# The attention's output bank in thirds, x turned by DMA, and the order of the instructions planned anew

## Chip, cores and metric

One core of one Trainium2 chip. The metric is the device time of one launch in microseconds (us); lower is better. TensorE is called PE (PEld its weight loads), VectorE DVE, ScalarE ACT, GpSimd POOL; SP issues most of the DMAs.

## What is computed

Attention with rotary positions for 4 batches x 8 heads, 576 positions and 64 values per head, then two layers with a gate between two products:

```python
q_rot, k_rot = (rotate(q), rotate(k))
scores = scale * np.matmul(q_rot, k_rot.transpose(0, 1, 3, 2))
attn = np.exp(scores - np.max(scores, axis=-1, keepdims=True))
attn = attn / (np.sum(attn, axis=-1, keepdims=True) + 1e-09)
x = np.matmul(attn, v)            # then heads side by side: 2304 tokens x 512
h = x @ w_in                      # layer 1: 512 -> 2048 -> 512
x = (h * np.clip(h + 3, 0, 6) / 6) @ w_out
h = x @ w_in2                     # layer 2: the gate is P(h) / (Q(h) + 1e-6)
out = g2(h) @ w_out2
```

To keep accuracy, float32 values are split into a high and a low float16 half in attention and layer 1 (high x high, high x low and low x high are multiplied), and into two float32r halves in layer 2.

## The kernel before, in words

**Attention.** The heads are taken in 16 pairs (4 batches of 4 pairs). A pair has five *units* (`unit`, line 820): four of 128 query rows for both heads, and a last one for the remaining 64 rows of each. A unit is a chain: PE makes the scores (L848) in one of two halves of a PSUM area; DVE takes the row maximum (L854); POOL or DVE scales it (L856); ACT takes exp in two calls (L861); POOL, ACT or DVE makes the high half p16h, DVE the low half p16l (L873); SP turns both by DMA transposes in blocks of 128 x 128 (L870), because the probabilities have to lie with the keys on the partitions; then PE multiplies them with V (L887 and L890, 30 matmuls, below called a P·V group). V has a column of ones, so that the sum of the row comes out as a 65th column. Both p16h and p16l have two buffers (`PR["p16"]`, L865).

**The output bank.** All P·V groups write the tile `ob`, one PSUM bank of 512 columns. Units are joined into *parts*: part 0 is the first two units of a pair, part 1 the other three. Unit n of a part writes 130 columns at n x 130, so a part fills up to 390. Beyond column 400 the same bank takes small products (L652, L760) that sum a column over the partitions, read by DVE (L599). When the last unit of a part is done, `x_out` (L894) normalises it: DVE makes the factor (L905), the divisor (L906) and its reciprocal (L908), and multiplies out of PSUM into the tile xn in SBUF (L910); PE transposes xn in 2 or 3 blocks into a PSUM tile `h` (L919, in float32, with the unit matrix); ACT or DVE makes the high half xt from it, DVE the low half (L923). The next part's P·V groups write the same columns, and the plan has them wait until L910 has read the bank:

```python
        op("P", c_pe(D + 1, 30), pv, r=[th, tlo, v9], w=[(ob, 0)])
```

**Layer 1** (`layer1`, L929) follows for each batch in the same two parts, 256 and 320 tokens: 16 groups of 12 matmuls (L953), with an elementwise chain on ACT, DVE (L957 to L962) and POOL or ACT for the high half, then 4 groups of 48 (L977), whose result goes to DRAM. Weights of layer 1 come in as float64 words and are decoded and split on ACT, DVE and POOL in the first 150 us; those of layer 2 are decoded later and kept in DRAM. **Layer 2** (L1114) starts when attention and layer 1 have given back their memory: five blocks of up to 512 tokens, matmuls at L1127 and L1160.

**The order.** Nothing is scheduled by the chip: each engine and each DMA queue works its own list in the order in which it was written. `Plan` collects all operations with the tiles they read and write, a cost per engine they may run on (`c_act`, `c_dve`, `c_pe`, ...), and a priority, which is a due time in ticks of 4 us plus an offset per tile name (`o_...`, in the first batch also `z_...` of the table `PR`). `order` (L388) then plays the kernel through with these costs, always giving a free engine the ready operation with the lowest priority; an engine that is not the first choice costs `pen` ticks. It counts time from an operation's end until another engine can start (L466), and `slack`. The dependences it knows go by tile and key: `(ob, 0)` and `(ob, 400)` are different keys. Waits on the chip are then put in for every conflict of what is read and written.

Of the kernel before, what the change touches and what calls it, by code (L numbers as in the profile page):

```python
# [22 lines left out]
S = 576  # L23
# [14 lines left out]
PR = {'c01': -12.485,  # L38
 'e': 2,
 'e_dec': 'GA',  # L40
 'e_dec0': 'DA',
 'e_gh': 'GD',
# [3 lines left out]
 'e_hi': 'GD',  # L46
# [5 lines left out]
 'e_qk0': 'GAD',  # L52
# [19 lines left out]
 'e_y': 'A',  # L72
# [33 lines left out]
 'o_hx': -0.79,
 'o_ident': 39.08,
 'o_k2': 11.91,
 'o_lgh': 7.11,
 'o_lgl': -78.93,  # L110
 'o_lq': -20.68,
 'o_lr': -7.59,
 'o_ls': 18.32,
 'o_lt': 5.34,
 'o_mx': 9.72,
 'o_na': 49.46,
 'o_nat': 8.34,
 'o_ob': -0.52,
 'o_ones': 50.39,
# [5 lines left out]
 'o_pw': 25.74,
 'o_pwi': -52.17,
 'o_qal': -12.64,
 'o_qam': -4.0,
 'o_qb': -50.8,
 'o_qk16': -0.86,  # L130
 'o_qpi': -2.45,
 'o_qps': 7.54,
 'o_qpv': -10.27,
 'o_r': -11.95,
# [4 lines left out]
 'o_s': -0.76,
 'o_so': -34.31,  # L140
 'o_t': -153.93,
 'o_t0': 16.25,
 'o_t1': 8.57,
 'o_tab': 0.98,
# [62 lines left out]
 'w20': 112.413,  # L207
 'w21': 133.738,
# [46 lines left out]
 'z_pth': 1.28,
 'z_ptl': -0.54,
 'z_pw': -13.15,
 'z_pwi': 41.55,
 'z_qal': -37.21,
 'z_qam': -53.51,  # L260
 'z_qb': -22.51,
 'z_qk16': 0.19,
 'z_qpi': -65.94,
# [4 lines left out]
 'z_raw': -17.19,
 'z_ropea': -4.31,
 'z_s': 29.8,  # L270
 'z_so': -1.68,
 'z_t': -7.2,
 'z_t0': 10.22,
 'z_t1': -8.07,
 'z_tab': -21.29,
# [238 lines left out]
def c_pe(n, passes):  # L514
    return passes * (n / 2.4 + 2.5)
# [741 lines left out]
```

## Time and profile before

| | |
|---|---|
| median of 3 runs | 1212.54 us (1210.96 to 1216.21) |
| the profiled execution | 1213.46 us, its span 1211.7 us |
| PE busy | 1021.2 us (84%) |
| DVE / ACT / POOL busy | 942.9 / 660.8 / 210.5 us |
| granted TensorE clock, mean | 0.932 of full |
| DMA | 137.72 MB, 276519 packets, 224192 of them under 512 B |

How to read it: the busy times are of one execution, the span runs from its first to its last instruction, and what lies between the span and its own time (1.8 us) is before and after. A wait is idle time of an engine just before an instruction, put down to what came last; idle time of an engine that sets no end costs nothing. [...] Landing is the time from issue to the last byte.

### The profile page before, as it was taken

Reading aid. Unit: us, or ns where it says so; the run is one execution under the profiler, and the core shown is the slowest. Engines: PE = TensorE matmul, PEld = TensorE weight load, DVE = VectorE, ACT = ScalarE, POOL = GpSimd, SP = SyncE. Lnnn points to the kernel's source line nnn. Section 1 sums busy time; section 2 is a strip of 40 time slices with the busy share of each in tenths; the row PEclk is TensorE's granted clock in tenths of the full one; section 3 lists DMA queues with packets and bytes.
Section 4 is the critical chain, followed back from the end, with each engine's and each line's share of the span. In section 5 each row is a group of like instructions: output and inputs, shape, how many; then the busy total and the mean of one; then the engine's idle time right before and its main releaser. Section 6 shows DMA issues by size and latency. Waiting matters only on the chain.

```text
span 1211.7 us, 21452 instructions
## 1 busy us (share of the span) xinstructions
PE 1021.2 (84%) x8182; PEld 810.7 (67%) x8182; DVE 942.9 (78%) x1697; ACT 660.8 (55%) x1183; POOL 210.5 (17%) x266
## 2 busy tenths in 40 slices
PE   0243589789889699798898998999999999999997
PEld 0122477666678467676666786777888888888895
DVE  5998798888686695796883854759989888887877
ACT  4665565553463362362441441467867667676676
POOL 0341353332130330241430420000000000000000
PEclk9955799899999699899899898999999999999999
DMA  7899765984997756878756844343010020010010
GB/s 215 215 233 231 158 157 124 159 170 99 191 157 166 142 100 148 165 158 183 142 117 145 165 107 101 114 147 93 9 48 23 1 52 10 1 35 10 1 36 18
DMA packets 276519, 137.72 MB, mean 114 GB/s; under 512 B 224192, under 2 KB 257600, under 8 KB 276416
## 3 DMA queue, kind: packets, MB, share of 16 engines
q1 hardware_dynamic: 270000, 127.91, 48.5%
q10 hardware_dynamic: 6416, 8.44, 2.5%
q8 instruction: 64, 1.05, 0.4%
q14 instruction: 39, 0.32, 0.1%
HBM read 61.33 MB, written 17.83 MB: 65 GB/s over the span
## 4 chain that ended last, share of the span: by engine, by line
PE 56%; DVE 19%; DMA 9%; issue 6%; ACT 6%; SPq 2%; POOL 2%; ACTq 0%; DVEq 0%; POOLq 0%
PE ac L1160 15%; PE h L977 9%; PE hh L1127 8%; PE h L953 7%; PE hx L1127 7%; PE s L848 5%; DVE mx L854 4%; ACT e L861 3%; DVE p16l L873 3%; DMA t<-qk 2%; PE ob L887 2%; DMA w2d<-f 2%; DVE gl L962 1%; DMA ptl<-p16l 1%; DVE t L959 1%
## 5 line engine op out<-in xcount | busy, mean ns | idle before, releaser
L953 PE MATMUL h<-xt,w 128*128 128x256 f16 (+1 forms) x1536 | 209.5, 293 | 8.3 <-DVE t L959 7.6
L953 PEld LDWEIGHTS <-w 128*128 128x128 f16 x1536 | 152.1, 101 | 53.3 <-issue 11.7
L977 PE MATMUL h<-gh,w 128*128 128x256 f16 (+1 forms) x960 | 185.3, 286 | 0.0
L1160 PE MATMUL ac<-w,lgh 128*128 128x512 f32 x576 | 179.8, 393 | 3.4 <-ACT lgh L1150 3.4
L861 ACT ACTIVATE e<-s,mx,qal 128x576 f32<-128x576 f32 (+1 forms) x144 | 116.0, 833 | 121.1 <-DVE mx L854 44.4
L977 PEld LDWEIGHTS <-w 128*128 128x128 f16 x1440 | 140.0, 98 | 35.0
L848 PE MATMUL s<-t,t 128*128 128x192 f16 (+10 forms) x360 | 91.5, 309 | 63.7 <-ACT e L861 37.0
L977 PE MATMUL h<-gl,w 128*128 128x256 f16 (+1 forms) x480 | 137.2, 286 | 0.0
L854 DVE TENSOR_REDUCE mx<-s 128x2 f32<-128x1152 f32 (+1 forms) x80 | 99.3, 1245 | 42.9 <-ACT e L861 21.6
L848 PEld LDWEIGHTS <-t 128*128 128x128 f16 (+1 forms) x720 | 64.0, 112 | 98.8 <-issue 57.0
L1160 PEld LDWEIGHTS ac<-w,lgh 128*128 128x128 f32 x576 | 107.1, 188 | 27.9 <-ACT lgh L1150 5.1
L1127 PE MATMUL hh<-x,w 128*128 128x512 f32 (+1 forms) x516 | 116.0, 374 | 0.0
L1160 PE MATMUL ac<-w,lgl 128*128 128x512 f32 x288 | 114.0, 396 | 1.3 <-DVE lgl L1151 1.2
L873 DVE TENSOR_TENSOR p16l<-e,p16h 128x1152 f16<-128x1152 f32 (+1 forms) x80 | 106.4, 1331 | 9.8 <-DMA ptl<-p16l 6.7
L957 ACT ACTIVATE t<-h,half,d 128x256 f32<-128x256 f32 (+1 forms) x128 | 75.1, 587 | 64.1 <-PE h L953 61.7
L1127 PEld LDWEIGHTS hh<-x,w 128*128 128x128 f32 x516 | 91.5, 189 | 19.6
L887 PE MATMUL ob<-v,pth 128*128 128x65 f16 (+1 forms) x800 | 81.5, 206 | 19.9 <-DVE xn L910 13.3
L1127 PE MATMUL hx<-x,w 128*128 128x512 f32 (+1 forms) x444 | 97.9, 369 | 0.0
L848 PE MATMUL s<-k,t 128*128 128x192 f16 (+10 forms) x360 | 88.7, 308 | 0.0
L1127 PEld LDWEIGHTS hx<-x,w 128*128 128x128 f32 x444 | 77.4, 188 | 16.3
L532 POOL TENSOR_SCALAR p16h<-e 128x1152 f16<-128x1152 f32 (+1 forms) x56 | 71.1, 1271 | 93.8 <-DMA pth<-p16h 65.2
L856 POOL TENSOR_SCALAR mx<-mx,qal 128x2 f32<-128x2 f32 (+1 forms) x76 | 42.0, 552 | 234.9 <-DVE mx L854 207.6
(135 smaller groups left out, 1939.6 us busy)
## 6 DMA issues: line engine op xcount, KB each, us to landing
raw<-in_moe_w_in_dram SPq DMA_DIRECT2D x32, 512.0 KB, 4.8
raw<-in_moe_w_out_dram SPq DMA_DIRECT2D x32, 512.0 KB, 4.2
w2d<-f SPq DMA_DIRECT2D x32, 256.0 KB, 4.5
w2s<-w2d SPq DMA_DIRECT2D x32, 256.0 KB, 2.7
out_dram<-ob SPq DMA_DIRECT2D x36, 128.0 KB, 2.4
vnat<-in_v_dram SPq DMA_DIRECT2D x16, 256.0 KB, 3.5
nat<-in_q_dram SPq DMA_DIRECT2D x32, 128.0 KB, 2.4
nat<-in_k_dram SPq DMA_DIRECT2D x32, 128.0 KB, 3.0
```

The source lines that it names most:

```text
L532: pool.tensor_scalar(out, in_, scale, 0.0, ALU.mult, ALU.add)
L848: pe.matmul(sbank()[r0:r0 + m, x:y], lhsT=qq[:, q0:q0 + m], rhs=kk[:, kx:kx + y - x], start=(j == 0), stop=(j == 1))
L854: op("D", c_dve(n), lambda e: vec.reduce_max(mx()[:, 0, 0:g], sv().rearrange("p (g n) -> p g n", g=g), axis=AX.X), r=[s], w=[(mx, 0)])
L856: op(EN("e_mx"), {"D": 170, "G": 270}, lambda e: EL[e].tensor_scalar(mx()[:, 1, 0:g], mx()[:, 0, 0:g], al()[:, 1:2], float(LSH * np.log(2. ...
L861: op("A", c_act(n // g, 2, False), lambda e, h=h: act.activation(et()[:, h * (n // g):(h + 1) * (n // g)], sv()[:, h * (n // g):(h + 1) * ...
L873: op(EN("lo"), c_sub(n), lambda e: EL[e].tensor_tensor(lo()[:, 0:n], et()[:, 0:n], ph()[:, 0:n], ALU.subtract), r=es + [ph], w=[lo])
L887: pe.matmul(ob()[0:m, o:o + D + 1], lhsT=w, rhs=vv[:, 0], start=(z == 0 and j == 0), stop=(z == 1 and j == 4))
L953: pe.matmul(hp()[:, 0:N], lhsT=w[:, z, kk], rhs=xt()[:, kk, 0:N], start=(n == 0), stop=(n == 11))
L957: op("A", c_act(N, 2, False), lambda e, t=t, hp=hp, f=f: act.activation(t()[:, 0:N], hp()[:, 0:N], AF.Relu, bias=half(), scale=d()[:, f:f ...
L977: pe.matmul(yp()[:, 0:N], lhsT=w[:, s_, m * 128:(m + 1) * 128], rhs=gt()[:, f, 0:N], start=(f == 0 and z == 0), stop=(f == KF - 1 and z == 2))
L1127: pe.matmul(hp()[:, 0:n], lhsT=w[:, kk], rhs=xt()[:, kk, 0:n], start=(i == 0), stop=(i == 11))
L1160: pe.matmul(accs[j][i]()[0:m], lhsT=gt()[:, x:x + m], rhs=wt(), start=(f == 0 and z == 0), stop=(f == KF - 1 and z == 2))
```

## The change

1. The thirds of the bank take turns over all units, `i % 3`, whichever part they belong to, and are three keys in the plan. After each P·V group the third is copied into an SBUF tile `xu` (new, two buffers, ACT or DVE).
2. `x_out` normalises `xu` in place in SBUF, makes high and low half there (high on ACT, low on DVE), and SP turns both by DMA transposes of 2 or 3 blocks straight into the tiles that layer 1 reads. The transposes on PE, the tile xn and the reading of `h` are gone.
3. p16l has one buffer (`'p16l': 1`), p16h keeps two.
4. The plan's costs: the time between engines falls from 200, 145, 130, 90 ns (P, A, D, G) to 190, 50, 60, 50 and `slack` from 80 to 40; small DVE operations are counted with 155 ns (before 60 to 90), small products with 330 (before 60), a matmul column with 1/2.34 ns (before 1/2.4).
5. The table `PR`: nearly all offsets and due times have other values (some 200 lines), `pen` falls from 23.2 to 7.9 ticks, and the engines allowed for some steps change.

```diff
-PR = {'c01': -12.485,
+PR = {'c01': -11.047,
...
+ 'e_ev': 'AD',
+ 'e_ev0': 'AD',
...
- 'e_hi': 'GD',
+ 'e_hi': 'GAD',
...
- 'e_w': 'GA',
+ 'e_w': 'G',
...
- 'e_xh': 'AD',
+ 'e_xh': 'A',
...
- 'e_y': 'A',
+ 'e_y': 'AD',
...
+ 'p16l': 1,
- 'pen': 23.208,
+ 'pen': 7.889,
...
- 'slack': 80,
+ 'slack': 40,
...
-                        end += (0 if o.dma else {"P": 200, "A": 145, "D": 130, "G": 90}.get(e, 0)) + PR["slack"] * (e != "N")
+                        end += (0 if o.dma else {"P": 190, "A": 50, "D": 60, "G": 50}.get(e, 0)) + PR["slack"] * (e != "N")
...
-    return passes * (n / 2.4 + 2.5)
+    return passes * (n / 2.34 + 2.5)
...
-    op("D", 140, lambda e: vec.memset(obank()[64:128, 4 * (D + 1):6 * (D + 1)], 1.0), w=[(obank, 0)])
...
-        ph, lo = (tl("attn", [128, 2 * S], F16, "p16" + z, PR["p16"]) for z in "hl")
+        ph, lo = (tl("attn", [128, 2 * S], F16, "p16" + z, n_) for z, n_ in (("h", PR["p16"]), ("l", PR["p16l"])))
...
-        o0 = (cc - 2 * part) * 2 * (D + 1)
+        o0 = i % 3 * 2 * (D + 1)
+        if cc == 2 * part:
+            xus[P, part] = tl("attn", [128, 3, 2, D + 1], F32, "xu", 2)
+        xu = xus[P, part]
...
-        op("P", c_pe(D + 1, 30), pv, r=[th, tlo, v9], w=[(ob, 0)])
+        op("P", c_pe(D + 1, 30), pv, r=[th, tlo, v9], w=[(ob, i % 3)])
+        op(EN("e_ev"), c_copy(2 * (D + 1), 0, False), lambda e: copy(
+            e, xu()[:, cc - 2 * part].rearrange("p h d -> p (h d)"), ob()[:, o0:o0 + 2 * (D + 1)]),
+           r=[(ob, i % 3)], w=[(xu, cc)])
...
-            xts[b_, part] = [tl("attn", [128, HP, PARTS[part][1]], F16, f"xt{part}{i}") for i in range(2)]
+            xts[b_, part] = [tl("attn", [128, HP, m * 128], F16, f"xt{part}{i}") for i in range(2)]
...
-            return obank()[:, 0:2 * m * (D + 1)].rearrange("p (j d) -> p j d", j=2 * m)
+            return xu()[:, 0:m].rearrange("p j h d -> p (j h) d")
...
-        xn = tl("attn", [128, 3, 2, D], F32, "xn")
         op("D", c_dve(m * 128), lambda e: vec.tensor_tensor(
-            xn()[:, 0:m].rearrange("p j h d -> p (j h) d"), ov()[:, :, 0:D],
-            r()[:, 0:2 * m].unsqueeze(2).to_broadcast([128, 2 * m, D]), ALU.mult), r=[(obank, 0), r], w=[xn])
-        tp = tl("psh", [128, 512], F32, "h", 2)
...
-                pe.transpose(tp()[:, 128 * j:128 * j + w], xn()[0:w, j].rearrange("p h d -> p (h d)"), ident()[0:w, 0:w])
-        op("P", 240 * m, turn, r=[xn, ident], w=[tp])
...
+            ov()[:, :, 0:D], ov()[:, :, 0:D], r()[:, 0:2 * m].unsqueeze(2).to_broadcast([128, 2 * m, D]), ALU.mult),
+           r=[r], w=[xu])
...
+        op(EN("e_xh"), c_copy(m * 128), lambda e: copy(e, xh()[:, 0:m], xn()[:, 0:m]), r=[xu], w=[xh])
+        op("D", c_dve(m * 128), lambda e: vec.tensor_tensor(xl()[:, 0:m], xn()[:, 0:m], xh()[:, 0:m], ALU.subtract),
+           r=[xu, xh], w=[xl])
+        for t, x in zip(xts[b_, part], (xh, xl)):
+            op("Q", (625, 189 * m, 1), lambda e, t=t, x=x: DE[e].dma_start_transpose(
+                out=t()[:, p].rearrange("p (j e) -> p j e", j=m), in_=x()[:, 0:m].rearrange("p j h d -> p (j h d)")),
+               r=[x], w=[(t, p)])
```

## Rows read from the trace of the kernel before

**Rows 1.** stages: stretch, PE, PEld, DVE, ACT, POOL, clock, DMA share, GB/s

```profile
0.00:150.00 150.00, 46.65 (x406) 33.42 (x407) 118.31 (x242) 84.61 (x170) 38.19 (x42) 0.75 0.86 211
...
150.00:745.00 595.00, 517.90 (x5574) 410.48 (x5570) 443.88 (x793) 261.69 (x440) 172.29 (x224) 0.93 0.72 148
...
745.00:1212.00 467.00, 456.67 (x2209) 366.82 (x2209) 380.72 (x663) 314.54 (x573) 0.00 (x0) 0.99 0.14 39
```

**Rows 2.** PE's waits, 150 to 745 us; columns: total us, times, longest us

```profile
PE s L848 <- ACT e L861: 31.1, 24, 3.6
...
PE h L919 <- DVE xn L910: 15.6, 8, 3.0
...
PE h L953 <- DVE t L959: 7.6, 14, 2.9
...
PE s L848 <- DVE mx L854: 5.9, 5, 2.3
```

**Rows 3.** waits of the whole run, two lines

```profile
PE ob L887 <- DVE xn L910: 13.3, 2, 11.1
...
DVE p16l L873 <- DMA ptl<-p16l: 6.7, 6, 3.0
```

**Rows 4.** busy time in ten-microsecond slices, columns as in rows 1

```profile
220.00:230.00 10.00, 6.68 (x81) 4.59 (x81) 7.05 (x12) 5.72 (x10) 3.43 (x4) 0.77 1.02 172
...
490.00:500.00 10.00, 5.45 (x77) 4.58 (x79) 7.14 (x16) 3.48 (x5) 1.68 (x3) 0.75 1.13 202
...
730.00:740.00 10.00, 5.68 (x115) 4.62 (x113) 5.02 (x9) 1.35 (x3) 0.00 (x0) 0.87 1.06 191
```

**Rows 5.** line 919, 150 to 745 us: PE, PEld, clock, DMA share, GB/s

```profile
150.00:745.00 595.00, 17.51 (x74) 9.93 (x74) 0.93 0.72 148
```

**Rows 6.** ACT groups by form: busy us, mean ns, idle before, releasers

```profile
L530 ACT ACTIVATE xt<-h 128x320 f16<-128x320 f32 x14 | 6.1, 434 | 20.7 <-PE h L919 20.7
...
L530 ACT ACTIVATE xt<-h 128x256 f16<-128x256 f32 x15 | 5.6, 380 | 12.1 <-PE h L919 11.3 <-ACT t L530 0.8
```

**Rows 7.** timeline around 233 us; start us, length us, engine, line, operation

```profile
232.99 0.28 PE L652 MATMUL ob<-qam,ones 128*128 128x2 f32 x2
...
233.26 1.36 DVE L854 TENSOR_REDUCE mx<-s 128x2 f32<-128x1152 f32 x1 [1.98 <-PE s L848]
...
234.53 0.15 DVE L599 TENSOR_SCALAR qpi<-ob 128x2 int32<-128x2 int32 x1
...
234.74 0.19 PE L887 MATMUL ob<-v,pth 128*64 128x65 f16 x1 [1.47 <-DVE qpi L599]
```

**Rows 8.** DMA, 150 to 745 us: packets, MB, share; count, us to landing

```profile
q1 hardware_dynamic: 209886, 81.41, 67.7%
...
ptl<-p16l SPq DMA_TRANSPOSE x71, 3.4
...
pth<-p16h SPq DMA_TRANSPOSE x70, 3.4
...
t<-qk SPq DMA_TRANSPOSE x24, 3.6
```

**Rows 9.** timeline at the end of the attention

```profile
742.57 0.47 PE L887 MATMUL ob<-v,ptl 128*64 128x65 f16 x5
...
743.56 0.56 DVE L910 TENSOR_TENSOR xn<-ob,r 128x384 f32<-128x384 f32 x1
...
745.15 1.25 PE L953 MATMUL h<-xt,w 128*128 128x320 f16 x4
```

**Rows 10.** groups by form, columns as in rows 6

```profile
L861 ACT ACTIVATE e<-s,mx,qal 128x576 f32<-128x576 f32 x128 | 101.9, 827 | 100.5 <-DVE mx L854 39.3 <-POOL mx L856 23.4 <-PE s L848 19.3
...
L873 DVE TENSOR_TENSOR p16l<-e,p16h 128x1152 f16<-128x1152 f32 x64 | 92.5, 1447 | 9.0 <-DMA ptl<-p16l 6.0 <-POOL p16h L532 2.9
...
L854 DVE TENSOR_REDUCE mx<-s 128x2 f32<-128x1152 f32 x64 | 86.3, 1351 | 36.2 <-ACT e L861 18.8 <-PE s L848 17.2
```

**Rows 11.** tile ptl; ns min/median/max, first and last start us

```profile
L870 SPq DMA_TRANSPOSE ptl<-p16l x80: 1199/1318/3033, 72.5 to 739.1; - x80
```

More of the change, by code (lines that the diff above doesn't have):

```diff
@@ L104 @@
- 'o_hh': 0.04,
+ 'o_half': 30.38,
+ 'o_hh': 3.47,
  'o_hr': 11.75,
[L106 to L119, printed above, removed]
+ 'o_hx': 2.9,
+ 'o_ident': 123.38,
+ 'o_k2': 20.73,
+ 'o_lgh': 20.57,
+ 'o_lgl': -106.78,
+ 'o_lq': -26.42,
+ 'o_lr': -17.86,
+ 'o_ls': -32.38,
+ 'o_lt': 4.62,
+ 'o_mx': 12.06,
+ 'o_na': 32.3,
@@ L120 @@
+ 'o_nat': 5.5,
+ 'o_ob': -0.02,
+ 'o_ones': 67.22,
  'o_p1': -5.5,
  'o_p16': 0.25,
- 'o_p16h': 26.14,
- 'o_p16l': 1.11,
+ 'o_p16h': 71.26,
+ 'o_p16l': 0.03,
  'o_pt': 6.74,
[L125 to L134, printed above, removed]
+ 'o_pth': -0.49,
+ 'o_ptl': -17.99,
+ 'o_pw': 29.19,
+ 'o_pwi': -70.51,
+ 'o_qal': -46.2,
+ 'o_qam': -19.48,
+ 'o_qb': -31.25,
+ 'o_qk16': -0.07,
@@ L135 @@
+ 'o_qpi': -4.09,
+ 'o_qps': 9.14,
+ 'o_qpv': -7.12,
+ 'o_r': -32.53,
  'o_r0': 18,
- 'o_raw': -6.9,
- 'o_ropea': 23.2,
+ 'o_raw': -4.69,
+ 'o_ropea': 21.79,
  'o_ropeb': 4.5,
[L139 to L144, printed above, removed]
+ 'o_s': -0.66,
+ 'o_so': -36.55,
+ 'o_t': -183.67,
+ 'o_t0': 24.37,
+ 'o_t1': 4.12,
+ 'o_tab': -100.57,
  'o_u': -23,
- 'o_v9': 15.2,
- 'o_vam': 96.81,
- 'o_vm4': 20.13,
+ 'o_v9': 26.5,
+ 'o_vam': 128.46,
+ 'o_vm4': 30.69,
@@ new lines @@
+ 'o_vnat1': -45.82,
+ 'o_vpi': 0.74,
+ 'o_vps': -80.53,
+ 'o_vpv': -86.81,
+ 'o_vqi': 6.66,
+ 'o_vqs': -33.57,
+ 'o_vqv': -8.27,
+ 'o_vv': -17.75,
+ 'o_w0_': 46.98,
+ 'o_w1_': 8.43,
+ 'o_w2_': 10.25,
+ 'o_w2d': 41.17,
+ 'o_w2s': -31.23,
+ 'o_wam': -30.75,
+ 'o_wao': 5.42,
+ 'o_woi': -102.96,
+ 'o_wos': -21.55,
+ 'o_wov': 35.51,
+ 'o_wpi': -122.42,
+ 'o_wps': -9.8,
+ 'o_x20': 55.75,
+ 'o_x21': -38.42,
+ 'o_xf': 11.87,
+ 'o_xh': -21.46,
+ 'o_xl': 14.9,
+ 'o_xn': -19.23,
+ 'o_xt': -5.19,
+ 'o_xu': -1.53,
@@ L250 @@
+ 'z_ident': 17.11,
+ 'z_k2': 67.02,
+ 'z_lgh': 21.26,
+ 'z_lgl': -86.27,
+ 'z_lq': -88.96,
+ 'z_lr': 2.57,
+ 'z_ls': -56.38,
+ 'z_lt': 26.3,
+ 'z_mx': 4.11,
+ 'z_na': -78.1,
+ 'z_nat': 13.08,
+ 'z_ob': -82.48,
+ 'z_ones': -10.77,
  'z_p1': -8,
  'z_p16': 1.15,
- 'z_p16h': -0.64,
- 'z_p16l': 14.9,
+ 'z_p16h': 4.66,
+ 'z_p16l': 16.99,
  'z_pt': -21.65,
[L255 to L263, printed above, removed]
@@ L264 @@
- 'z_qps': 16.33,
- 'z_qpv': -95.54,
- 'z_r': -17.58,
- 'z_r0': -13.5,
[L268 to L275, printed above, removed]
+ 'z_pth': -7.52,
+ 'z_ptl': -10.93,
+ 'z_pw': 5.48,
+ 'z_pwi': 42.46,
+ 'z_qal': -137.42,
+ 'z_qam': -59.51,
+ 'z_qb': -6.54,
+ 'z_qk16': -3.05,
+ 'z_qpi': -116.91,
+ 'z_qps': 43.07,
+ 'z_qpv': -153.21,
+ 'z_r': -14.14,
+ 'z_r0': -13.5,
+ 'z_raw': -25.27,
+ 'z_ropea': -39.82,
+ 'z_s': 50.81,
@@ L297 @@
[L297 to L308 removed]
+ 'z_vnat0': 14.67,
+ 'z_vnat1': -4.91,
+ 'z_vpi': -64.07,
+ 'z_vps': -88.99,
+ 'z_vpv': -17.0,
+ 'z_vqi': -6.8,
+ 'z_vqs': -20.25,
+ 'z_vqv': -27.71,
+ 'z_vv': 0.25,
+ 'z_w0_': -66.99,
+ 'z_w1_': 3.99,
+ 'z_w2_': 116.31,
+ 'z_w2d': 44.8,
+ 'z_w2s': -0.93,
+ 'z_wam': 10.77,
+ 'z_wao': -31.51,
@@ L309 @@
+ 'z_woi': 40.4,
+ 'z_wos': 32.62,
+ 'z_wov': 48.37,
+ 'z_wpi': -11.61,
+ 'z_wps': -93.05,
+ 'z_x20': 5.77,
+ 'z_x21': -88.6,
+ 'z_xf': -5.22,
+ 'z_xh': 5.58,
+ 'z_xl': 0.44,
+ 'z_xn': -41.77,
+ 'z_xt': -84.47,
+ 'z_xu': 7.8,
  'z_y0': -3.5,
- 'z_y1': -26.49,
- 'z_y1d': 49.55}
+ 'z_y1': -65.72,
+ 'z_y1d': 55.58}
 def cls(nm):
@@ L755, in turned @@
             return sbank()[0:HP, 2432:2560]
-        op("P", 110, lambda e: pe.transpose(turned(), am(), ident()), r=[ident] + [(am, p) for p in range(HP)], w=[ps])
+        op("P", 330, lambda e: pe.transpose(turned(), am(), ident()), r=[ident] + [(am, p) for p in range(HP)], w=[ps])
         m4 = tl("attn", [HP, 1], F32, "vm4", 2)
```

231 lines of the change are left out of this document (83 added, 148 removed).

## Prediction

> **What bounds the kernel now.** I read the views in this order: busy time by stage, who PE waits for, the costly groups by form, and two short timelines.
>
> By stage [rows 1]: for the first 150 us PE works 46.65 us, and DVE (118.31 of 150) with the DMA engines (0.86) sets the pace. From 150 to 745 us attention and layer 1 are interleaved, and PE is busy 517.90 of 595 us. From 745 us PE hardly stops (456.67 of 467): the last part of layer 1, then layer 2, which the change leaves as it is but for its order. So what the change can win or lose lies mostly in 150 to 745 us. [...]
>
> PE's named waits in this stretch [rows 2] are mostly matters of order (scores behind exp 31.1 us, behind the row maximum 5.9, layer 1 behind its elementwise step 7.6), but 15.6 us are transposes of x waiting for the normalised block. P·V groups wait for the same reading of the bank twice, 13.3 us in all, 11.1 of them in one wait at the start and 2.2 later [rows 3].
>
> The second bound is the DMA engines. In the ten-microsecond slices at 490 and 730 us they are at 1.13 and 1.06 (queues overlap, so the share passes 1), and PE falls to 5.45 and 5.68 of 10 us and to a clock of 0.75 and 0.87 [rows 4]. Twelve slices in this stretch, from the one at 220 to that at 730 us, have a share of 0.99 or more; in them PE is busy 70% on average, 87% over the whole stretch. Transposes by DMA are the load there.
>
> **The change part by part.** The sum is made against the profiled execution: 1213.5 us, of which the span is 1211.7. The median of the runs is 0.9 us below it.
>
> *Transposes leave PE (gain 15).* 80 transposes go, 74 of them after 150 us, 17.51 us of PE time [rows 5]. PE is busy 87% of that stretch, so I count 15 us; at least 0, where PE would have waited anyway, at most 17.5.
>
> *Waits for the normalised block go (gain 14).* Of the 15.6 us before the transposes I take half, 8, since PE's next work may be late too. Of the P·V waits I take 2.2 and a third of the 11.1 of the start, together 6; DVE and DMA pace the start. Ends for the two: 4 and 29.
>
> *The copy-out of each block (cost 9).* 80 copies of 130 columns from PSUM are new. ACT takes 380 ns for 256 columns and 434 ns for 320, which a line carries to 0.27 us at 130 [rows 6]. ACT is busy 262 of 595 us [rows 1] and has the room. The cost is the wait it puts on PE. A timeline shows it: PE ended a two-column product in the bank at 233.27; the P·V group behind it, in other columns, started at 234.74, when DVE, after 1.36 us of another reduction, had made its 0.15 us read of those two columns [rows 7]. So the bank behaves as one thing: a read of one third will hold the P·V group of the next, and a copy waits for a P·V group in flight. With a quarter of the 80 copies having a P·V group right behind, at 0.27 plus some 0.18 between engines, that is 9 us. On ACT a copy that waits for its group holds the exps behind it, and with them DVE's low halves; ACT's idle half covers that. Ends: 0 and 80 x 0.45 = 36.
>
> [...]
>
> *x turned by DMA (cost 8).* 64 transposes of 2 or 3 blocks, 160 blocks of 32.8 KB, 5.2 MB, go onto the SP queue among 192. From 745 us on, with plain transfers alone, 0.14 of 467 us carried 39 GB/s, 3.6 us of all 16 engines per MB [rows 1]. In 150 to 745 us the SP queue used 67.7% for 81.41 MB, 4.9 us per MB [rows 8]; about 45 MB of that are transposes (71 and 70 of the probabilities' halves, on average 8.2 blocks, and 24 of q and k with 9), and with the rest at 3.6 they come to 6.0. So the new load is 19 to 31 us of DMA time; I take 31, as the price of the same operation. It hurts where DMA is already full, in 120 of 595 us, and a little beside: a quarter, 8 us. Ends: 0 and 31. On SP the new ones cost issue time too, at 1.2 us at least for 5 or 9 blocks [rows 11] some 77 us beside the 250 of the 192 others, over 745 us; each waits there for its half of x, and behind it stand the units' own transposes and the loads. The plan puts the half before it, so I charge nothing more; if a fifth of that queue time reached PE it would be the upper end over again.
>
> [...]
>
> *The last x (cost 4).* At the end the last P·V group ends at 743.04 and layer 1 starts at 745.15, 2.1 us later [rows 9]. Afterwards the way is: copy 0.27, two small steps 0.2 each, normalise 0.56, high half on ACT about 0.5 (0.43 for 320 columns [rows 6]), low half on DVE as long as the normalising, some 0.15 between each two, and a DMA transpose of 3.4 us to landing [rows 8]: 6.4 us, 4 more. Ends 0 (other layer 1 work kept back as cover) and 6. For the 31 x parts before it, layer 1 is placed about two ticks of 4 us later than the attention it feeds, and other PE work covers the wait.
>
> *Everything else (gain 18).* The order itself is planned anew, from longer durations for small instructions and shorter hops between engines, with hundreds of changed offsets. Nothing in the trace of before prices that. [...] From 745 us on PE is full but for 10 us [rows 1]: nothing.
>
> Small edits: one memset at the start goes, nothing; DVE's normalise and low half keep their sizes; the high half moves to ACT, which has 333 us idle in the stretch. Without that cover each would cost 0.5 us, 16 in all.
>
> Sum: 1213.5 - 15 - 14 + 9 + 8 + 4 - 18 = 1187.5; with the 0.9 us between this execution and the median, **1187 us**.
>
> **The rivals.**
>
> *The single buffer for the low half decides: slower.* The low half of the probabilities goes from two buffers to one. A write of 1.45 us on DVE, two hops and a transpose of 3.4 us to landing [rows 8, 10] put the low transposes of two units at least 5.0 us apart. In the trace of before 33 of the 79 gaps between one such transpose and the next are shorter, the missing time adding up to 56 us (80 transposes, from 72.5 to 739.1 us [rows 11]). DVE issues in order, so a write that waits holds the row maximum and all that exp and the scores wait for. It decides from the point where half of the 56 us reach PE, 28, and the new order wins nothing, 18: 1187 + 46 = 1233. For it: the ACT-behind-maximum and scores-behind-exp chains are already the longest waits. Against it: DVE is idle for 151 us of the stretch, and the units come on average 8 us apart.
>
> *The thirds are not thirds: no change.* The bank is one for its readers and writers, as above, so the change does not do what it says. If a third of the copies stand behind one exp (0.83) or one maximum (1.35) [rows 10] with a P·V group waiting, 27 at 1.1 us are 29 in place of 9: 1207. For it: the 1.47 us seen. Against it: before, the bank was held through four DVE steps in each of 32 places, and that summed to only 13.3 us.
>
> [...]
>
> **How the numbers follow.** A measurement of this kernel can tell 0.5%, 6 us, from no change. Forecast 0.50 (1174 to 1203), single buffer 0.17, one bank 0.13, much better order 0.20. The outer cases reach from 1153 to 1230, which leaves out about 2 in 10. Faster by more than 0.5% (below 1206.5): nearly all of the forecast, the better order and a part of the one-bank case, 0.70; same 0.12; slower 0.18.
>
> **What would show it.** The transposes and their waits are gone from PE, and from 150 us to the start of layer 2 it takes 25 us less. The copies take 0.25 to 0.3 us, and P·V groups wait for them 5 to 15 us in all. The share of DMA rises by about 0.05 and the transposes of x take some 3.4 us to land. DVE's wait for the transpose of the low half, 6.7 us now [rows 3], stays below 20. Wrong it would be if that wait were 40 us or more, if layer 1 waited for x in many places, or if layer 2 were the part that changed.

## The result and the profile after

The changed kernel takes 1166.8 us (1164.3 to 1171.7) against 1212.2 beside it: a ratio of 0.9625, 95% interval 0.9586 to 0.9663, a gain of 45 us where 25 were forecast. It lies in the range (1153 to 1230) and below the 1174 to 1203 that the likeliest case alone was given; the forecast's 1187 is 20 us above it, the lower end of the range 14 below.

The busy time by stage, cut as in [rows 1] (columns as there):

```profile
0.00:150.00 150.00, 39.59 (x293) 27.78 (x294) 114.91 (x241) 79.18 (x163) 36.27 (x43) 0.70 0.79 201
150.00:745.00 595.00, 541.18 (x5930) 427.39 (x5930) 476.93 (x881) 309.83 (x532) 191.18 (x229) 0.97 0.82 165
745.00:1170.00 425.00, 408.88 (x1880) 332.46 (x1878) 354.78 (x602) 297.33 (x539) 0.00 (x0) 0.99 0.13 34
```

The gain is where it was looked for. From 150 to 745 us PE is busy 541 us in place of 518 at a clock of 0.97 in place of 0.93, so more of layer 1 and 2 is done by 745 us and what is left takes 420 us, 47 less. The share of the DMA engines rises by 0.10 (0.05 was forecast). The first 150 us hold less PE work than before, 39.6 in place of 46.7.

PE's waits from 150 to 745 us, against [rows 2] (total us, times, longest us):

```profile
PE s L854 <- ACT e L867: 14.5, 10, 5.2
PE s L854 <- DVE mx L860: 11.7, 7, 6.2
PE ob L896 <- DMA ptl<-p16l: 9.7, 10, 3.0
PE h L966 <- DVE t L972: 7.5, 11, 1.4
```

Scores behind exp fell from 31.1 to 14.5 us, the 15.6 us before the transposes are gone, scores behind the maximum rose from 5.9 to 11.7, and a wait that was small is now third: P·V for the transposed low half. Over the whole run, against [rows 3], the low half waits for its one buffer, and P·V for a copy-out once:

```profile
DVE p16l L879 <- DMA ptl<-p16l: 19.5, 14, 5.2
PE ob L896 <- DMA ptl<-p16l: 17.4, 13, 5.4
...
PE ob L896 <- ACT xu L537: 1.1, 1, 1.1
```

In the slices that stood for the DMA limit in [rows 4] PE now works 9.4 us or more, at a clock of 1.00 and with the DMA engines below 1 (other work stands there now; the last one is behind the attention). It is not only where queues overlap that the share passes 1: before, in the slice at 490 us, queue 1 alone had 112.7%; at 730 us it had 100.9% and queue 10 another 4.9%. The three slices of after:

```profile
220.00:230.00 10.00, 9.80 (x120) 8.27 (x118) 8.29 (x23) 6.79 (x12) 2.61 (x6) 1.00 0.82 132
490.00:500.00 10.00, 9.44 (x120) 6.87 (x118) 6.24 (x12) 5.76 (x9) 1.38 (x2) 1.00 0.86 177
730.00:740.00 10.00, 10.00 (x75) 7.20 (x74) 6.65 (x13) 6.54 (x12) 0.00 (x0) 1.00 0.93 322
```

The slices with a DMA share of 0.99 or more are now others, and again twelve between 150 and 745 us. PE is busy 92% in them, where it was 70% before; two of them:

```profile
480.00:490.00 10.00, 10.00 (x100) 7.60 (x98) 9.50 (x16) 5.44 (x10) 1.82 (x1) 1.00 1.05 204
...
670.00:680.00 10.00, 9.99 (x133) 8.70 (x132) 8.38 (x17) 4.63 (x9) 4.34 (x5) 1.00 1.17 239
```

So full DMA engines were not what held PE back in the twelve slices of before, or not they alone.

The new operations by tile (ns min/median/max, first and last start), the copies first, then the transposes of x, with PE's waits before the matmuls that read them and the time to landing:

```profile
L537 ACT ACTIVATE xu<-ob x47: 258/279/288, 84.1 to 684.3; 128x130 f32<-128x130 f32 x47
L541 DVE COPY xu<-ob x33: 274/286/294, 115.8 to 689.5; 128x130 f32<-128x130 f32 x33
```

```profile
L935 SPq DMA_TRANSPOSE xt<-xh x32: 1167/1207/2104, 123.5 to 692.2; - x32
...
  DVE t L972: 7.5, 11
  ACT t L537: 0.5, 1
...
DMA to landing us min/median/max: 2.3/2.4/5.2
```

A copy takes 0.28 us (0.27 forecast), on ACT 47 times and on DVE 33. The transposes land after 2.4 us (3.4 forecast). No matmul of layer 1 waits for x. At the end, against [rows 9], the last block is copied at 689.5 us and the last half of x issued at 694.4 us:

```profile
689.54 0.29 DVE L541 COPY xu<-ob 128x130 f32<-128x130 f32 x1 [6.36 <-PE ob L896]
...
694.40 1.23 SPq L935 DMA_TRANSPOSE xt<-xl  x1
```

and layer 1's last matmuls on x start at 724.7 us (its line in the same view of the tile); other layer 1 work lies between.

### The profile page after: what moved, and what is told of

Same layout as the page of the kernel before. It is cut to its first block, busy times and chain, and to the rows that moved or that the text cites. A ratio compares the mean times of both kernels' runs of the same rounds, so it can differ in the third digit from the quotient of the medians.

```text
span 1165.1 us, 21501 instructions
## 1 busy us (share of the span) xinstructions
PE 989.7 (85%) x8102; PEld 787.6 (68%) x8102; DVE 946.6 (81%) x1721; ACT 686.3 (59%) x1233; POOL 227.4 (20%) x271
## 2 busy tenths in 40 slices
DMA packets 299048, 142.97 MB, mean 123 GB/s; under 512 B 246720, under 2 KB 280128, under 8 KB 298944
## 4 chain that ended last, share of the span: by engine, by line
PE 53%; DVE 20%; DMA 10%; ACT 6%; issue 5%; SPq 3%; POOL 2%; ACTq 0%; DVEq 0%; POOLq 0%
PE ac L1173 15%; PE h L990 9%; PE hh L1140 9%; PE hx L1140 7%; PE h L966 7%; DMA ptl<-p16l 5%; DVE mx L860 4%; PE s L854 4%; DVE p16l L879 3%; ACT e L867 3%; DMA t<-qk 2%; PE ob L896 2%; DVE w L644 1%; DVE t L972 1%; DVE gl L975 1%
## 5 line engine op out<-in xcount | busy, mean ns | idle before, releaser
L966 PE MATMUL h<-xt,w 128*128 128x256 f16 (+1 forms) x1536 | 202.7, 287 | 8.6 <-DVE t L972 7.5
L990 PE MATMUL h<-gh,w 128*128 128x256 f16 (+1 forms) x960 | 190.6, 287 | 0.0
L966 PEld LDWEIGHTS <-w 128*128 128x128 f16 x1536 | 148.5, 98 | 49.6 <-issue 11.5
L990 PEld LDWEIGHTS <-w 128*128 128x128 f16 x1440 | 139.3, 99 | 35.2 <-issue 0.3
L854 PE MATMUL s<-t,t 128*128 128x192 f16 (+9 forms) x360 | 88.3, 300 | 65.8 <-DMA t<-qk 28.9
L860 DVE TENSOR_REDUCE mx<-s 128x2 f32<-128x1152 f32 (+1 forms) x80 | 99.4, 1245 | 38.0 <-PE s L854 19.8
L854 PEld LDWEIGHTS <-t 128*128 128x128 f16 (+1 forms) x720 | 61.6, 109 | 100.6 <-issue 43.3
L879 DVE TENSOR_TENSOR p16l<-e,p16h 128x1152 f16<-128x1152 f32 (+1 forms) x80 | 101.2, 1265 | 20.6 <-DMA ptl<-p16l 19.5
L1140 PEld LDWEIGHTS hh<-x,w 128*128 128x128 f32 x516 | 92.0, 190 | 23.2 <-DVE lt L1155 3.9
L970 ACT ACTIVATE t<-h,half,d 128x256 f32<-128x256 f32 (+1 forms) x128 | 74.9, 587 | 47.7 <-PE h L966 46.7
L539 POOL TENSOR_SCALAR gh<-t 128x256 f16<-128x256 f32 (+1 forms) x95 | 66.2, 698 | 148.6 <-DVE t L972 143.7
L862 POOL TENSOR_SCALAR mx<-mx,qal 128x2 f32<-128x2 f32 (+1 forms) x75 | 53.4, 712 | 203.3 <-DVE mx L860 140.2
L854 PE MATMUL s<-k,t 128*128 128x192 f16 (+9 forms) x360 | 85.2, 299 | 0.0
L896 PE MATMUL ob<-v,pth 128*128 128x65 f16 (+1 forms) x800 | 77.1, 200 | 7.2 <-DMA pth<-p16h 3.3
```

The lines of the kernel that those rows point to most:

```text
L539: pool.tensor_scalar(out, in_, scale, 0.0, ALU.mult, ALU.add)
L854: pe.matmul(sbank()[r0:r0 + m, x:y], lhsT=qq[:, q0:q0 + m], rhs=kk[:, kx:kx + y - x], start=(j == 0), stop=(j == 1))
L860: op("D", c_dve(n), lambda e: vec.reduce_max(mx()[:, 0, 0:g], sv().rearrange("p (g n) -> p g n", g=g), axis=AX.X), r=[s], w=[(mx, 0)])
L862: op(EN("e_mx"), {"D": 170, "G": 270}, lambda e: EL[e].tensor_scalar(mx()[:, 1, 0:g], mx()[:, 0, 0:g], al()[:, 1:2], float(LSH * np.log(2. ...
L879: op(EN("lo"), c_sub(n), lambda e: EL[e].tensor_tensor(lo()[:, 0:n], et()[:, 0:n], ph()[:, 0:n], ALU.subtract), r=es + [ph], w=[lo])
L896: pe.matmul(ob()[0:m, o:o + D + 1], lhsT=w, rhs=vv[:, 0], start=(z == 0 and j == 0), stop=(z == 1 and j == 4))
```

## The experiments

Two kinds were run. In the first kind, whose names begin with x, the order is held: an operation that two kernels share keeps the start time that the planner of one of them gave it, and the issue order of every engine follows these times; an operation whose predecessors come later is put off until they are issued. How well that holds an order can be read from the traces: against before, x_one_lo, x_thirds1 and x_parts have at most 21 of PE's some 8,100 matmuls and 16 of DVE's operations in another place; against after, x_copy2 and x_no_low have none of PE's, but x_order has 1686. The edit is the same in all of them:

```diff
-    res = pl.order()
-    for o, e in res:
+    pl.order()
+    for o, e in by(pl, TIMES):
         o.fn(e)
```

In the second kind the kernel's own planner plans again. But for after_nudged, the offsets in PR are searched anew as well, by random steps on the planned length and with as many tries for each. How long the order of the change itself was searched is not on record, so its search may have been the better one.

### The new code in the old order

x_parts is the code after with the times of before; new operations stand 0.2 us behind what they read.

> All of the new code (thirds, copy-out, normalising in place, x turned by DMA, one low buffer) in the order of the kernel before: every operation that both kernels have keeps its planned place, a copy-out is put 0.2 us behind its P.V group, a transpose of x 0.2 us behind its half. Theory A (the forecast's sum: the parts are worth -15 -14 +9 +8 +4 = -8 us, the order the rest of the 45 us): 1204 us, ratio 0.993. Theory B (the parts are most of the gain, and the new order only follows from them): 1180 or less, 0.973. Theory C (the single low buffer costs in an order that was not made for it): 1225 or more, 1.01, with DVE waiting over 30 us for the low half's transpose.

Measured: 1399.6 us, ratio 1.153 (1.149 to 1.156). Theories A and B fail. Theory C (1225 or more) holds, and its sign is there, DVE waiting 174.0 us for the low half (its line is below), though nobody put a price like this on it: the parts alone, unplanned, cost 185 us.

x_order is the reverse, the code before with the times of after.

> The code of the kernel before (bank held until x is normalised, transposes of x on PE, two low buffers) in the order of the kernel after: every operation that both have is issued in the planned place of the new kernel, the PE transposes right behind their normalising step. Theory A (parts worth 8 us, order the rest): 1175 us, ratio 0.969. Theory B (the new order is worth nothing without the parts): 1205 or more, ratio 0.994 or more, with P.V groups and transposes waiting for the normalised block 30 us or more. A result between says how much of the order's gain needs the parts.

Measured: 1382.3 us, ratio 1.138 (1.135 to 1.141). That is theory B, far beyond its price, with its sign: transposes wait 26.5 and P·V groups 14.2 us for the normalised block. It is not the pure order of after: 1200 of the 1686 matmuls in another place belong to P·V groups, which had to be put off because the bank is held for a whole part. In x_order the engines stand in line for the bank and for the transposed x:

```profile
ACT xt L530 <- PE h L919: 71.9, 24, 10.9
...
DVE r L906 <- PE ob L887: 60.1, 16, 6.8
...
PE h L919 <- DVE xn L910: 26.5, 14, 4.2
```

### One low buffer, and the copies, in the old order

x_one_lo changes one thing of the kernel before:

```diff
-        ph, lo = (tl("attn", [128, 2 * S], F16, "p16" + z, PR["p16"]) for z in "hl")
+        ph, lo = (tl("attn", [128, 2 * S], F16, "p16" + z, n_) for z, n_ in (("h", PR["p16"]), ("l", 1)))
```

> The kernel before in its own order, with one buffer in place of two for the low half of the probabilities. Forecast (the wait mostly falls into DVE's idle time): 1212 to 1218 us, ratio 1.000 to 1.005, DVE waiting 15 to 25 us for the low half's transpose. The rival of the single buffer (33 of 79 gaps too short, half of the missing 56 us reach PE): 1240, ratio 1.023, and a wait of 40 us or more.

Measured: 1335.8 us, ratio 1.099 (1.095 to 1.104): 121 us more. DVE's wait for the buffer, 6.7 us in [rows 3], is now

```profile
DVE p16l L873 <- DMA ptl<-p16l: 125.0, 45, 6.2
```

So the rival of the single buffer had the mechanism right and its price too low, for an order that was not made for it. A likely reason, which no run isolates: the 56 us that were missing between transposes were counted unit by unit, but a DVE that stands still delays the next unit's maximum, exps and transposes too. In the order of after DVE waits 19.5 us for the same buffer.

x_thirds1 adds the thirds and the copies to it:

> The kernel before in its own order with one low buffer, and with the bank in thirds and each block copied out by ACT; x is still turned on PE. Against x_one_lo: theory A (copies cost 9 us on PE's P.V groups, of the waits of P.V for the bank 6 us go): 3 us more, ratio 1.002 to 1.003. Bank as one thing (27 copies at 1.1 us hold P.V): 20 us or more over x_one_lo, with P.V waiting 25 us or more for ACT's copies. Copies free: 6 us less than x_one_lo.

Measured: 1336.6 us, ratio 1.101 (1.098 to 1.105), 2 us over x_one_lo by the ratios, give or take 7. So copies and thirds together cost less than some 9 us there, and the case of the bank as one thing (20 us or more, with P·V waiting 25) is out: P·V groups wait 4.9 us for ACT's copies. The forecast's 3 us and nothing are both left. The step from here to x_parts, 63 us, is x turned by DMA in an order without room for it; there P·V waits for the copies, layer 1 for x, and DVE longer still for the low half:

```profile
DVE p16l L879 <- DMA ptl<-p16l: 174.0, 49, 6.7
...
PE ob L896 <- ACT xu L537: 20.4, 6, 9.6
...
PE h L966 <- DMA xt<-xh: 17.7, 5, 7.8
```

### What a copy and a transpose of x cost in the new order

x_copy2 copies each block twice:

```diff
+        op(EN("e_ev"), c_copy(2 * (D + 1), 0, False), lambda e: copy(
+            e, xu()[:, cc - 2 * part].rearrange("p h d -> p (h d)"), ob()[:, o0:o0 + 2 * (D + 1)]),
+           r=[(ob, i % 3)], w=[(xu, cc)], key=f"ev{P}_{cc}")
```

(`key` names an operation in the list of held times.)

> The kernel after in its own order, with each block copied out twice (80 more copies of 128x130 right behind the first, same engine, same target). Forecast's price (a quarter of the copies have a P.V group right behind and hold it): 6 us more than the kernel after, 1173. By the one wait of 1.1 us that PE showed for a copy: 0 to 2 us more, 1168. The bank as one thing: 20 us or more, 1187.

Measured: 1169.8 us, ratio 0.9636 (0.9604 to 0.9669): by the ratios 1.3 us more than the kernel after, give or take 6. Twenty are excluded; the forecast's 6 are not quite. The trace of after says why it is small. During none of the 80 copies was PE writing in the bank, and only twice did its next product there start within half a microsecond of a copy's end; the forecast had a quarter of them, 20. One was a P·V group, at 106.2 us. The other was a small product, in the timeline at 330 us (start us, length us; in brackets the wait and who ended it):

```profile
330.18 0.28 DVE L541 COPY xu<-ob 128x130 f32<-128x130 f32 x1
...
330.62 0.35 PE L658 MATMUL ob<-qam,ones 128*128 128x2 f32 x2 [0.82 <-DVE xu L541]
```

And a copy waits for products in other columns of the bank, here over the whole run (total us, times, longest us):

```profile
ACT xu L537 <- PE ob L658: 10.8, 6, 3.9
```

So the bank is still one thing for its users, as [rows 7] had it: in the trace of after, up to 745 us, none of the 2603 recorded operations of PE, ACT and DVE on it overlaps one of another engine. What would happen if they did, no run here shows. What is smaller than forecast is how often a P·V group meets a copy. Why is not shown: the plan holds the thirds under three keys, so it does not keep a copy away from the next group on purpose, and 80 groups in 610 us leave room between them.

x_no_low leaves out the transposes of x's low half, so the high half stands in its place:

```diff
-        for t, x in zip(xts[b_, part], (xh, xl)):
+        for t, x in zip(xts[b_, part], (xh,)):
...
-                for z, xt in ((0, xh), (0, xl), (1, xh)):
+                for z, xt in ((0, xh), (0, xh), (1, xh)):
...
-            op("P", c_pe(N, 12), mm, r=[xh, xl, wt], w=[hp])
+            op("P", c_pe(N, 12), mm, r=[xh, wt], w=[hp])
```

> The kernel after in its own order without the 32 transposes of x's low half; layer 1's matmuls for that half read the high half in its place (as many matmuls of the same size), so the part of x's low half is left out of the result. Forecast's price (8 us for 64 transposes): 4 us less than the kernel after, 1163. If the transposes are hidden: no change, 1167. If they cost the upper end (31 us for all): 15 us less, 1152.

Measured: 1161.5 us, ratio 0.9563 (0.9532 to 0.9594): 7.5 us less by the ratios, give or take 6. That is 15 for all 64 if the other half costs the same: the forecast's 8 is within the uncertainty, hidden transposes (0) and the upper end (31) are not, the first by little. The work on DMA has a price, and the forecast was right to charge it.

### The place of layer 1

x_after_l1b moves layer 1's 832 operations, with P·V groups for a clock, to where they stood before.

> The kernel after, with layer 1's operations alone moved to where they stood in the kernel before, counted in P.V groups (2 to 4 groups earlier in most places, the same pace otherwise); all else keeps its order. Theory D (the new place and even pace of layer 1 are what fills PE and keeps its clock up): 15 to 30 us slower than the kernel after, 1182 to 1197, the granted clock from 200 to 700 us at 0.93 to 0.95 in place of 0.99. Theory E (the gain is in attention's own waits, layer 1's place matters little): within 6 us of 1167, clock as before.

Measured: 1347.6 us, ratio 1.110 (1.106 to 1.114). That is far beyond theory D too, and it settles nothing on the place of layer 1: with its operations up to 8 groups earlier in every engine's queue, half of them by 2 to 4, attention's own steps stand behind them (scores behind exp 47.3 us, the maximum behind exp 61.0 on DVE). Like the runs above, it shows one order moved in part, and at a high price.

### Each part alone, planned anew

Three codes, planned from the durations of the kernel after and searched alike. r_order is the code before. r_thirds has the thirds, the copies and one low buffer, with x turned on PE. r_xdma has x turned by DMA and one low buffer, with the bank held whole and no copies.

```diff
-        op("P", 240 * m, turn, r=[xn, ident], w=[tp])
...
+        for t, x in zip(xts[b_, part], (xh, xl)):
+            op("Q", (625, 189 * m, 1), lambda e, t=t, x=x: DE[e].dma_start_transpose(
+                out=t()[:, p].rearrange("p (j e) -> p j e", j=m), in_=x()[:, 0:m].rearrange("p j h d -> p (j h d)")),
+               r=[x], w=[(t, p)], key=f"dx{P}_{part}_" + ("h" if x is xh else "l"))
```

> The code of the kernel before, planned from the durations of the kernel after, its offsets searched anew (as many tries as for the two runs beside it): the change's order part alone. Theory F (the order is worth the 37 us that the sum leaves to it): 1175, ratio 0.97. Theory G (a new order is worth little without the parts, because transposes and waits for the normalised block stay on PE): 1200 to 1220, ratio 0.99 to 1.005.

> Thirds, copy-out and one low buffer, but x still turned on PE; planned from the durations of the kernel after, offsets searched anew. If the bank's hold was what the old order suffered from: 1175 to 1185, ratio 0.97 to 0.975. If the thirds carry only the small waits of P.V (6 us against 1 us for the copies): as r_order, 5 us to either side.

> x turned by DMA and one low buffer, but the bank held whole until x is normalised, no copies; planned from the durations of the kernel after, offsets searched anew. If x by DMA carries the change (18 us of PE work, their waits, and room for the order): 1165 to 1180, ratio 0.96 to 0.973, 20 us or more below r_order. If the thirds carry it: as r_order.

Measured: r_order 1200.0 us, ratio 0.986 (0.983 to 0.990); r_thirds 1189.2, 0.979 (0.977 to 0.981); r_xdma 1171.3, 0.962 (0.958 to 0.967). Theory G holds for r_order, at its edge, and F does not; r_thirds lies between its two forecasts; r_xdma is as forecast if x by DMA carries the change, 29 us below r_order. The kernel with x by DMA and no thirds is as fast as the change.

r_two_lo is r_xdma with the second low buffer back, with three buffers in place of four for some small tiles to make room:

> As r_xdma, but with two buffers for the low half of the probabilities, as in the kernel before; offsets searched anew with as many tries. If the single buffer still costs in an order that was made for it (5 to 20 us): 1152 to 1166. If the searched order puts its cost away: within 6 us of r_xdma's 1171, with DVE's wait for the low half's transpose falling from some 15 to 20 us to under 8 without any gain.

Measured: 1193.1 us, ratio 0.982 (0.980 to 0.985), 22 us slower than r_xdma, which neither forecast had. DVE's wait for the low half's transpose, 10.2 us in r_xdma, is not in its list any more, and nothing is gained by it. But for the planner's numbers the two codes differ in these buffers alone, and PE's busy time is the same within 2 us, so what differs is most likely the order that the search found; that fewer small buffers cost something is not excluded. The difference lies between 150 and 690 us, where PE is idle 73 us in place of 51, in scores that wait (150 to 690 us, r_xdma first, then r_two_lo):

```profile
PE s L855 <- ACT e L868: 22.6, 15, 5.1
...
PE s L855 <- DVE mx L861: 3.6, 5, 1.4
```

```profile
PE s L855 <- ACT e L868: 28.4, 18, 6.6
PE s L855 <- DVE mx L861: 17.3, 14, 4.2
```

after_nudged is the kernel after with one number of its planner changed:

```diff
- 'slack': 40,
+ 'slack': 44,
```

> The kernel after with one number of its planner nudged (the slack that is added to every operation, 44 ns in place of 40), so the same code in a neighbouring order that was not searched. If the gain lies in the code and a rough order will do: within 6 us of 1167. If the order has to fit in every place: 20 us or more slower, 1187 or more.

Measured: 1202.1 us, ratio 0.990 (0.987 to 0.993). That is the second forecast. Of the gain 12 us are left, with operations that are the same line for line in a plan that was not searched. The plan is another one all the same: 1550 of PE's 8102 matmuls and a third of DVE's operations stand in another place. Yet from 150 to 690 us PE is busy 484 of 540 us, about as long as the 486 of after; then layer 2's first matmuls wait, most of it in one place:

```profile
PE hh L1140 <- DVE lt L1155: 26.0, 2, 24.3
```

So two orders of nearly the same code lie 22 us apart (r_xdma and r_two_lo) and of the same code 35 us (after and after_nudged). No code was searched twice, so how far two searches of one code differ was not measured; the three times above rank the parts only roughly. More can be told from PE's busy time. The span of a profile is PE's busy time and its idle time (line 1 of the page for r_order, r_thirds, r_xdma, x_parts and x_after_l1b in turn):

```profile
PE 1016.7 (85%) x8182; PEld 809.7 (68%) x8182; DVE 949.1 (79%) x1716; ACT 668.3 (56%) x1181; POOL 213.3 (18%) x249
```

```profile
PE 1006.3 (85%) x8182; PEld 797.2 (67%) x8182; DVE 945.2 (80%) x1702; ACT 685.6 (58%) x1264; POOL 220.5 (19%) x260
```

```profile
PE 988.5 (84%) x8102; PEld 789.1 (67%) x8102; DVE 936.6 (80%) x1694; ACT 676.3 (58%) x1185; POOL 229.9 (20%) x267
```

```profile
PE 1052.6 (75%) x8102; PEld 824.1 (59%) x8102; DVE 934.8 (67%) x1696; ACT 680.8 (49%) x1263; POOL 203.2 (15%) x266
```

```profile
PE 1045.0 (78%) x8102; PEld 822.3 (61%) x8102; DVE 947.3 (70%) x1721; ACT 690.4 (51%) x1241; POOL 218.4 (16%) x263
```

What the transposes of x take of it is the busy time of their line, before, in r_order and in r_thirds:

```profile
L919 PE MATMUL h<-ident,xn 128*128 128x128 f32 (+1 forms) x80 | 19.8, 333 | 19.2 <-DVE xn L910 19.2
```

```profile
L919 PE MATMUL h<-ident,xn 128*128 128x128 f32 (+1 forms) x80 | 19.0, 322 | 17.1 <-DVE xn L910 14.7 <-DVE vqs L603 1.8 <-DVE qpi L599 0.6
```

```profile
L933 PE MATMUL h<-ident,xn 128*128 128x128 f32 (+1 forms) x80 | 18.0, 307 | 15.4 <-DVE xn L924 14.2 <-DVE vqi L606 0.9 <-ACT t L537 0.3
```

| kernel | span | PE busy | of it transposes of x | PE busy without them | PE idle |
|---|---|---|---|---|---|
| before | 1211.7 | 1021.2 | 19.8 | 1001.4 | 190.5 |
| r_order | 1198.1 | 1016.7 | 19.0 | 997.7 | 181.4 |
| r_thirds | 1187.7 | 1006.3 | 18.0 | 988.3 | 181.4 |
| r_xdma | 1170.3 | 988.5 | 0 | 988.5 | 181.8 |
| r_two_lo | 1193.7 | 990.8 | 0 | 990.8 | 202.9 |
| after_nudged | 1200.4 | 996.2 | 0 | 996.2 | 204.2 |
| after | 1165.1 | 989.7 | 0 | 989.7 | 175.4 |
| x_after_l1b | 1345.3 | 1045.0 | 0 | 1045.0 | 300.3 |
| x_parts | 1401.4 | 1052.6 | 0 | 1052.6 | 348.8 |

The transposes of x are 18 to 20 us of PE's busy time wherever PE does them in a planned order. What is left, the same 8102 matmuls in every row, takes 988 to 1001 us in the planned orders and 1045 to 1053 in the last two, which moved operations to places planned for another kernel: it depends on the order, not on how x is turned (r_thirds and r_xdma are alike in it). The idle time of the planned kernels, 175 to 204 us, is the order's too: the two of the same code, after and after_nudged, are as far apart as any. From before to after PE's busy time falls by 31.5 us and its idle time by 15.1.

## Why the prediction was right, and where it was off

**Where to look, and the direction.** The gain lies in the stretch that the forecast named: layer 1's last matmul ends at 756.6 us in place of 798.7, 42 earlier, and what follows takes 408.5 us in place of 413.0. The two stalls it wanted gone are gone.

**Transposes leave PE: put at 15, worth 20.** The forecast took 87% of 17.5 us. All 80 transposes were 19.8 us of PE's busy time, and PE's whole idle time did not grow by them: it is 181.4 us in r_order and 181.8 in r_xdma. The forecast also counted only those after 150 us.

**The clock: no term of the sum, worth some 12.** Of the 31.5 us that PE is less busy, 11.7 are left when the transposes are taken off: the same matmuls take less time, and from 150 to 745 us the granted clock is 0.97 in place of 0.93. Of the 595 microseconds there it stood at 1.00 throughout in 503 before and in 556 after, at 0.50 in 69 and in 33. The hundred microseconds from 200 and from 400 us, of before and after, and those from 200 us of r_thirds, columns as in [rows 1]:

```profile
200.00:300.00 100.00, 85.80 (x858) 64.64 (x857) 87.23 (x144) 48.81 (x82) 32.12 (x40) 0.95 0.69 141
...
400.00:500.00 100.00, 84.00 (x800) 61.12 (x801) 71.02 (x124) 42.35 (x72) 26.53 (x31) 0.89 0.69 140
```

```profile
200.00:300.00 100.00, 91.85 (x1061) 73.81 (x1061) 89.59 (x161) 57.55 (x107) 41.55 (x48) 1.00 0.81 147
...
400.00:500.00 100.00, 95.45 (x1056) 72.76 (x1054) 83.02 (x156) 55.78 (x95) 28.57 (x32) 1.00 0.85 169
```

```profile
200.00:300.00 100.00, 90.91 (x999) 70.54 (x997) 87.78 (x153) 52.86 (x100) 40.47 (x47) 0.93 0.64 124
```

Before and after, the fuller stretch has the higher clock, but no rule follows from such means: r_thirds is at 0.93 with PE nearly as busy as in after. Nor is the clock a gift of x by DMA alone. r_thirds, with x still on PE, has its other matmuls done in 988.3 us, r_xdma in 988.5, r_order in 997.7: the time comes with the order, and which trait of an order brings it is not shown. This is the largest miss in the direction of the gain: a clock of 0.93 over 595 us [rows 1] costs, by an estimate, 42 us at most (0.07 of 595), and the sum has no term for it.

**The copies: put at 9, worth 1 to 2.** The bank behaves as assumed: ACT's copies waited for products in other columns 6 times, 10.8 us in all. The number of meetings was not as assumed: 2, not 20, and PE's waits in them were 1.1 and 0.8 us, together 1.9; a second set of copies cost 1.3 us, give or take 6. A meeting is dearer than the 0.45 us assumed, because PE had begun to wait before the copy began. From the copy's end to PE's start it took 0.05 and 0.15 us in them; in the trace of before it took 0.03 us from PE to DVE (at 743.04) and 0.14 from DVE to PE (at 744.12), together about the 0.18 between engines that the forecast estimated. The share of copies "with a P·V group right behind" was guessed in place of being counted. The second rival (27 copies at 1.1 us) falls with it, though its price for one was the better one.

**x turned by DMA: put at 8, by one half of it 15, give or take 12.** The 7.5 us of the low half are doubled here, which no run checks. Bytes were right (137.72 MB became 142.97), the landing was shorter than thought. The argument behind the 8, that it hurts where the DMA engines are full, is not borne out: in the twelve full slices of after PE is busy 92%. How the 7.5 us come about is open. Whether a transpose takes 6.0 us of DMA time per MB, as the forecast charged, or the 3.6 of the plain transfers (a quarter of 31 or of 19 us, so 8 or 5), this measurement does not tell.

**Waits for the normalised block: put at 14, gone, but not from the total.** The searched pair shows it best, since the code differs in little else (the second low buffer), but it is one pair. Its stages, r_order first, then r_xdma, columns as in [rows 1]:

```profile
0.00:150.00 150.00, 48.36 (x395) 33.99 (x397) 120.08 (x244) 89.70 (x174) 36.40 (x41) 0.72 0.85 211
150.00:690.00 540.00, 475.56 (x5125) 376.62 (x5122) 424.50 (x774) 246.16 (x417) 172.51 (x202) 0.95 0.75 154
```

```profile
0.00:150.00 150.00, 35.26 (x259) 24.64 (x259) 111.86 (x224) 73.72 (x151) 42.03 (x44) 0.73 0.79 196
150.00:690.00 540.00, 488.53 (x5565) 390.36 (x5566) 431.68 (x791) 279.93 (x454) 185.44 (x220) 0.96 0.84 163
```

From 150 to 690 us PE is idle 51 us in place of 64, 13 less and close to the 14. In the first 150 us it is idle 115 us in place of 102, 13 more, and it gets through less of the attention: 50 matmuls in place of 80 on the line below, that is 5 P·V groups in place of 8 (0 to 150 us, r_order, then r_xdma; busy us, mean ns):

```profile
L890 PE MATMUL ob<-v,pth 128*128 128x64 f16 x80 | 10.0, 231 | 0.0
```

```profile
L897 PE MATMUL ob<-v,pth 128*128 128x64 f16 x50 | 6.8, 244 | 0.0
```

Layer 1 then starts on PE at 192 us in place of 154. The idle time of the whole run is 181 to 182 us in both. The forecast had nothing for the slower start; the kernel after shares it (39.6 us of PE work in place of 46.7, layer 1 at 189.5 us in place of 151.1). What slows the start is not shown.

**The last x: put at 4, worth nothing that shows.** No matmul of layer 1 waits for it; layer 1's other work is the cover, the lower end of that term.

**The order: put at 18.** No run shows these 18 us as a term of their own; r_order, the order alone, is worth 16.6 us (0.0137 of 1214.8), give or take 4 from the measurement; the scatter between searched orders is larger than the term. That the size came out is luck: 18 is 40% of PE's three waits of order in [rows 2] (31.1, 5.9 and 7.6 us), and in r_order these three are 43.8 us from 150 to 745 us, against 44.6 before. That the parts can be priced at all in a fixed order and the order added on top was wrong as a picture: in the old order they cost 185 us. The sum can be held against the result only because its terms were prices in an order made for them.

**The single low buffer.** It did not decide: DVE's wait of 19.5 us is just under the 20 given as the line. But the case was nearer than its chance of 0.17 said: in the order of before it costs 121 us, not 28 to 56, and what averts it is an order planned for it. That the new order would do so was argued only from DVE's idle time and the units' mean distance. (By the start times in the trace the short gaps are 34 and the missing time 54 us, in place of 33 and 56; nothing hangs on that.)

In sum the forecast had PE's busy time 15 us lower and its idle time some 11 lower; measured are 31.5 and 15.1. The terms that were off are thus the transposes (15 for 20), the clock (nothing for 12) and some 11 us of costs (copies, last x) that found cover; against them stand the 14 us of waits that did not leave the total. So the direction was argued soundly, and the idle part of the sum came out close by errors that cancel. Shown is that some 20 of the 45 us are transposes that left PE. The rest, clock and idle time, hangs on the order: after_nudged has x by DMA, thirds and one buffer, and 12 us of gain. Not settled is how much the thirds are worth. r_thirds is 11 us below r_order, r_xdma without thirds is as fast as the change, and both differences are smaller than the 22 and 35 us between orders of nearly the same code. Thirds, x by DMA and two low buffers together were not run.

## What to carry to other kernels

Split a span into the bound engine's busy time and its idle time before pricing a change. Work that leaves the engine left the total here, 18 to 20 us among planned orders. What the clock gives back, and the waits, belong to the order: the same matmuls took 988 to 1053 us, and a wait that was taken away in one stretch stood in another. In a kernel whose order is searched, a part can be compared only with an order planned for it, and even then one order against another says little below some 20 us, so several searches of each code are needed, which these runs do not have. What to test first after such a change is the neighbouring order: here 4 ns in one planner number cost 35 us, most of it in one stall at the seam of two layers.

## What was not expected

- One buffer less for a tile of 2.3 KB per partition cost 121 us in an order made for two (1335.8 against 1214.3), with 125.0 us of waiting on DVE.
- Putting operations in places that were planned for another kernel cost 168 us and more (x_parts, x_order, x_after_l1b); adding 80 copies behind existing ones cost 1.3 us, give or take 6. And with an order held almost unchanged, one dependence more (x_one_lo) cost 121 us.
- The twelve slices with the fullest DMA engines had PE busy 70% before and 92% after: a full DMA share beside an idle PE was no proof that DMA was the bound.
- The DMA transposes of x, of 2 or 3 blocks, land after 2.4 us at a DMA share of 0.82, while those of the probabilities, 5 or 9 blocks, went from 3.4 us [rows 8] to 3.7 and 3.8:

```profile
pth<-p16h SPq DMA_TRANSPOSE x80, 3.8
ptl<-p16l SPq DMA_TRANSPOSE x80, 3.7
```
